# A transformer block in one kernel: the first token loads split over two queues, key rows set by GpSimd, the second root's order, and the last output columns in two parts

## The chip, the cores and the metric

The kernel runs on one core of a Trainium2 chip. A core has five engines that run side by side and wait for each other through semaphores: TensorE (PE; its weight loads are listed as PEld), VectorE (DVE), ScalarE (ACT), GpSimd (POOL) and SyncE (SP), which here only issues transfers. SP and ACT each have a DMA queue of their own. The metric is the device time of one execution in microseconds.

## The reference

The input x has 2048 tokens of 512 values. Two branches read its layer norm: attention over a sliding window, and a gated feed-forward network. The output is x plus the product of the first and the silu of the second.

```python
xn = _layernorm(x)                                # over the 512 values of a token
qkv = (xn @ wqkv)                                 # 32 heads of 16, window of 256 tokens
s = softmax(mask(q @ k.T / 4)) @ v  @ wo
h = silu(xn @ w1) * (xn @ w3)                     # 1792 wide
g = silu(h @ w2)
out = x + s * g
```

## The kernel before

The 2048 tokens are worked in four tiles of 512. Every float32 matrix is split into a high and a low float16 part, and a product is made of three float16 matmuls (high by high, high by low, low by high); weights are first scaled per matrix by a power of two that comes from their sum of squares. Scores and values work on small PE tiles, the feed-forward part on 128x128 tiles.

What runs when is decided in two steps. The Python code writes all instructions in one order. Then `listed` takes them as a list, estimates how long each takes, and gives every engine (PE, DVE, ACT, POOL, SP) an order of its own; the instructions up to `tc.settled`, which is set after the first projections, keep their written order on PE, DVE and ACT. So a change at the start moves instructions of the other engines in many later places, and PE's hardly at all, since its stream follows the written blocks.

The opening, before the dense stream begins, is what the change touches. Four blocks of 128 tokens (slots 0 to 3) are loaded, blocks 0 and 2 on SP's queue, 1 and 3 on ACT's, and behind them SP issues the first weights: the key part and the query part for the first eight heads (L386), the same for the next eight, the value weights (L346) and gate and up weights (L943). PE runs 22 dummy matmuls meanwhile (`keep_busy`, L1499). For each block DVE takes the statistics (`gather0`, L483, and `average0`, L486); for two blocks together ACT takes a root and DVE its reciprocal (`root01`, `invert01`, `root23`, `invert23`: L511, L515, L516, L517) and DVE refines it (L520, L521). `centre0` (L525) subtracts the mean and scales, `turn0` (L541) transposes on PE, and ACT and DVE make the parts XH and XL of it (L546, L551). For the first weights ACT squares the key part and then the query part with a sum along each row (`square`, L403), POOL casts the sums (L406), PE adds them over the partitions (`add_squares`, L420), DVE makes the scale (`inverse`, L425 to L427), and ACT makes the high parts (L410, the tile whi). With XH and whi the first real matmuls begin (`project`, L652). The second eight heads' weights take the same way by L249, L261, L276, L287, L294, L297 and L322; the value weights by L249, L251, L322 and L323 (wvh, wvl) to L619.

The KA tiles hold the keys of a tile, with rows of a constant; before, DVE fills KA[0], ACT fills KA[1] by one activation (L1476), and POOL fills KA[2] (L1491). At the very end `total_by_columns` makes the last 128 tokens' output in two halves of 256 columns: twelve matmuls each (L1321), then two DVE operations (L1323, L1324) and a store (L1325).

Transfers tell of their landing by eight semaphores, DMAHW0 to DMAHW7, that the compiled program uses in turn: an issue whose semaphore is still in use by a transfer eight places earlier waits until that one has landed.

Of the kernel before, what the change touches and what calls it, by code (L numbers as in the profile page):

```python
# [10 lines left out]
F32 = mybir.dt.float32  # L11
# [3 lines left out]
AF = mybir.ActivationFunctionType  # L15
# [6 lines left out]
P = 128  # L22
# [9 lines left out]
TW = S // NT  # L32
# [14 lines left out]
ONE = 2.0**12  # L47

TWO_ONES = struct.unpack("f", struct.pack("ee", -ONE, -ONE))[0]
# [44 lines left out]
def tile_block(ctx: ExitStack, tc: tile.TileContext, x, wqkv, wo, w1, w3, w2, out):  # L94
    nc = tc.nc
    x = x.flatten_outer_dims()
# [26 lines left out]
    def take(dtype):  # L123
        free.sort()
        slot = free.pop(0)[2]
        made = fpool.tile([P, 512 if dtype == F32 else 1024], dtype, name=slot, tag=slot, bufs=1)
        held[id(made)] = slot, made
        return made

    def give(*tiles, after=0):  # L130

        for made in tiles:
            given[0] += 1
            free.append((now[0] + after, given[0], held.pop(id(made))[0]))
# [38 lines left out]
    def bank(shape, dtype=F32):  # L173

        open_bank[0] = b = 1 - open_bank[0]
        return psm.tile(shape, dtype, name=f"m{b}", tag=f"m{b}", bufs=1)
# [24 lines left out]
    onesb = const.tile([P, P], BF16, name="onesb")  # L201
# [30 lines left out]
    KA = [const.tile([P, 4, KW], F16, name=f"KA{r}") for r in range(3)]  # L232
# [235 lines left out]
    def prepare(t):  # L468
# [3 lines left out]
        xts = {}  # L472
        pair = [None]

        def load(b):
            xts[b] = take(F32)
            (nc.scalar if t == 0 and b % 2 else nc.sync).dma_start(xts[b], x[t * TW + b * P:t * TW + (b + 1) * P, :])

        sts = {}

# [75 lines left out]
        def turn_beside(b, k0, k1, s, at=WIN):  # L556
# [17 lines left out]
            def rest():  # L574
# [5 lines left out]
                if whole:  # L580
                    turned[t] = turned.get(t, 0) + 1
            return rest
        return load, (gather, average) if t == 0 else stats, rstd if t == 0 else rstd_beside, centre, turn if t == 0 else turn_beside

    def prepare_beside(t, more=0):
# [659 lines left out]
    def gated(t, b):  # L1245


        if (t, b) in ACC and not isinstance(ACC[t, b], list):
            acc = ACC[t, b]
            y = take(F32)  # L1250
            nc.scalar.activation(y, acc, AF.Tanh, scale=0.5)
            nc.vector.scalar_tensor_tensor(y, y, 1.0, acc, op0=ALU.add, op1=ALU.mult)
            give(acc)
            return [y[:, 0:256], y[:, 256:512]], [y]
        h = b // 2
        if b % 2 == 0:
            GATED[t, h] = []
            for acc in HALF.pop((t, h)):
                y = take(F32)
                nc.scalar.activation(y, acc, AF.Tanh, scale=0.5)  # L1260
                nc.vector.scalar_tensor_tensor(y, y, 1.0, acc, op0=ALU.add, op1=ALU.mult)
                give(acc)
                GATED[t, h].append(y)
        ys = GATED[t, h]
        return [y[:, 256 * (b % 2):256 * (b % 2) + 256] for y in ys], ys if b % 2 else []
# [44 lines left out]
    def total_by_columns(t, b):  # L1310

        r = slice(t * TW + b * P, t * TW + (b + 1) * P)
        tb = slice(b * P, (b + 1) * P)
        WOH, WOL = SQ["wo"][:2]
        xr = XR[t, b]
        ys, done = gated(t, b)
        for c, y in zip((slice(0, 256), slice(256, 512)), ys):
            ps = bank([P, 256])
            for g in range(NG):
                for i, (a, w) in enumerate(((0, WOH), (0, WOL), (1, WOH))):  # L1320
                    nc.tensor.matmul(ps, O[t, g][:, a, tb], w[g][:, c], start=g == 0 and i == 0,  # L1321
                                     stop=g == NG - 1 and i == 2)
            nc.vector.scalar_tensor_tensor(y, ps, sc["y"], y, op0=ALU.mult, op1=ALU.mult)  # L1323
            nc.vector.tensor_add(y, y, xr[:, c])  # L1324
            nc.sync.dma_start(out[r, c], y)  # L1325
        give(*done, xr)
# [140 lines left out]
    load0, stats0, rstd0, centre0, turn0 = prepare(0)  # L1467
# [3 lines left out]
    for b in range(4):  # L1471
# [1 line left out]

    nc.scalar.activation(KA[1][:, 0, 0:1], eps, AF.Sqrt, bias=eps)
    nc.vector.memset(KA[0].rearrange("p a c -> p (a c)").bitcast(F32), TWO_ONES)
    nc.scalar.activation(KA[1].rearrange("p a (b c) -> p (a b) c", c=P), onesb.unsqueeze(1).to_broadcast([P, 24, P]),  # L1476
                         AF.Copy, scale=-ONE)
    qk[0][0]()
    qk[1][0]()
    wv[0]()  # L1480
# [6 lines left out]
    load(0, 3)  # L1487

    nc.gpsimd.memset(V[:, :, H * VW:], 0.0)
    for a in range(4):  # L1490
        nc.gpsimd.memset(KA[2][:, a, :].bitcast(F32), TWO_ONES)  # L1491


    spare = pso.tile([P, 2, TW], F32, name="po")
# [6 lines left out]
    gather0, average0 = stats0  # L1501
    root01, invert01, refine01 = rstd0(0, 2)
    root23, invert23, refine23 = rstd0(2, 4)
# [8 lines left out]
    root01()  # L1512
    gather0(2)
    invert01()
    square(0)
    gather0(3)
    average0(2)
    average0(3)
    root23()
    square(1)  # L1520
    refine01()
    centre0(0)
    copies.append(turn0(0))
    invert23()
    add_squares()
    centre0(1)
    copies.append(turn0(1))
    copies[0][0]()
    refine23()
# [69 lines left out]
    for n in range(len(units)):  # L1599
        t = n // 8  # L1600
# [7 lines left out]
        b = n % 8 - (2 if t == 1 else 4)  # L1608
# [28 lines left out]
    for b in range(4):  # L1637
        if b < 2:
            residual(NT - 1, b + 2)
        if b < 3:  # L1640
            run(total(NT - 1, b))
    total_by_columns(NT - 1, 3)
    flush()

# [419 lines left out]
```

## Time and profile before

| what | value |
|---|---|
| median of 3 runs (lowest, highest) | 793.35 us (793.29, 794.3) |
| the profiled execution's own time | 793.33 us |
| its span in the profile | 791.5 us |
| PE busy | 784.8 us, 99% of the span |
| DVE, ACT, POOL busy | 563.0, 453.3, 383.0 us |
| granted clock of PE over the span | 1.00 |
| moved by DMA | 121.94 MB, mean 154 GB/s |

The span runs from the first to the last instruction; 1.83 us of the profiled time lie around it. A row of the timeline reads: start in us, duration in us, engine, line, operation, out<-in, shape, count, and in brackets how long the engine had been idle and who ended that. A queue's own instructions are SPq and ACTq. An engine that is 99% busy here leaves 6.7 us that are not PE's, and they lie at the two ends.

### The profile page before, as it was taken

The numbers are of one execution on the slowest core, as the hardware profiler recorded it, in microseconds if no ns is written. First come the engines' busy times: TensorE is split into PE (matmuls) and PEld (weight loads), VectorE is DVE, ScalarE is ACT, GpSimd is POOL, SyncE is SP. The second block draws the span as 40 slices with busy tenths as digits, with TensorE's granted clock in tenths as the row PEclk, the third lists the DMA queues.
The fourth block names the chain that finished last, engine by engine and source line by source line (L and its number), as shares of the span: only waits on it lengthen the run. The fifth ranks groups of instructions, "written<-read, shape, count | busy, mean of one in ns | idle before, by whom it ended". The sixth has DMA issues, their size and how long they took to land.

```text
span 791.5 us, 23612 instructions
## 1 busy us (share of the span) xinstructions
PE 784.8 (99%) x9292; PEld 420.6 (53%) x9292; DVE 563.0 (71%) x1348; ACT 453.3 (57%) x754; POOL 383.0 (48%) x679
## 2 busy tenths in 40 slices
PE   8999999999999999999999999999999999999998
PEld 4444445444455554465556555445555555545554
DVE  8787787689667767788668766776767777676536
ACT  7999989757447655544354455644434356654411
POOL 2258858967527334516144633423152456544352
PEclk9999999999999999999999999999999999999999
DMA  9988775474863643556454543527464564225521
GB/s 285 278 242 230 244 216 163 122 206 138 249 174 111 166 133 87 150 163 156 125 148 127 168 117 98 141 66 184 123 178 124 146 180 113 59 93 169 166 68 54
DMA packets 112752, 121.94 MB, mean 154 GB/s; under 512 B 18432, under 2 KB 76928, under 8 KB 112640
## 3 DMA queue, kind: packets, MB, share of 16 engines
q1 hardware_dynamic: 112352, 119.90, 53.9%
q8 instruction: 73, 1.20, 0.7%
q10 hardware_dynamic: 288, 0.52, 0.2%
q14 instruction: 39, 0.32, 0.1%
HBM read 83.76 MB, written 32.37 MB: 147 GB/s over the span
## 4 chain that ended last, share of the span: by engine, by line
PE 95%; ACT 3%; DMA 1%; DVE 1%; issue 0%; SPq 0%; POOL 0%; ACTq 0%
PE m L1105 36%; PE m L1208 11%; PE m L652 10%; PE po L872 9%; PE m L1155 6%; PE s L844 6%; PE m L619 5%; PE m L1286 5%; PE po L752 2%; PE s L752 2%; DMA slot<-in_A_wqkv_dram 1%; PE s L706 1%; ACT slot L331 1%; PE s L652 1%; ACT slot L332 1%; ACT pt L854 1%
## 5 line engine op out<-in xcount | busy, mean ns | idle before, releaser
L1105 PE MATMUL m<-XH,slot 128*128 128x512 f16 x896 | 267.3, 380 | 0.0
L854 ACT ACTIVATE pt<-s,es 128x1024 f32<-128x1024 f32 x152 | 167.1, 1113 | 125.8 <-DVE s L851 124.0
L1105 PEld LDWEIGHTS <-slot 128*128 128x128 f16 x1344 | 125.0, 98 | 149.4 <-issue 9.2
L328 POOL TENSOR_TENSOR slot<-slot,slot 128x256 f16<-128x256 f32 (+1 forms) x222 | 150.0, 701 | 94.7 <-ACT slot L332 37.4
L1105 PE MATMUL m<-XL,slot 128*128 128x512 f16 x448 | 169.8, 379 | 0.0
L851 DVE TENSOR_TENSOR s<-s,MK 128x256 f32<-128x256 f32 (+2 forms) x280 | 119.3, 436 | 67.4 <-PE s L844 57.6
L1074 POOL TENSOR_TENSOR slot<-slot,slot 128x256 f16<-128x256 f32 x133 | 86.2, 671 | 49.7 <-ACT slot L1070 47.3
L1208 PE MATMUL m<-slot,slot 128*128 128x256 f16 x798 | 94.0, 273 | 0.0
L1208 PEld LDWEIGHTS <-slot 128*128 128x128 f16 x798 | 75.8, 98 | 15.1 <-issue 3.2
L872 PE MATMUL po<-pt,V 64*32 64x320 f32 (+4 forms) x2880 | 77.7, 344 | 0.0
L872 PEld LDWEIGHTS po<-pt,V 64*32 64x32 f32 x2880 | 51.8, 106 | 23.7 <-PE s L752 3.3
L1125 DVE SCALAR_TENSOR_TENSOR slot<-m,slot 128x512 f32<-128x512 f32 x56 | 38.4, 685 | 28.6 <-PE m L1105 28.4
L1116 ACT ACTIVATE slot<-m,sgs 128x512 f32<-128x512 f32 x56 | 38.4, 685 | 34.5 <-PE m L1105 34.4
L844 PEld LDWEIGHTS <-KA 50*64 50x64 f16 x1472 | 34.1, 106 | 42.7 <-issue 38.7
L1070 ACT CAST slot<-slot 128x512 f16<-128x512 f32 (+1 forms) x76 | 41.8, 565 | 24.3 <-DVE slot L1125 19.7
L844 PE MATMUL s<-qa,KA 50*64 50x320 f16 (+3 forms) x1472 | 53.9, 258 | 0.4 <-ACT pt L854 0.4
L1120 DVE SCALAR_TENSOR_TENSOR slot<-slot,m 128x512 f32<-128x512 f32 x56 | 38.2, 682 | 19.9 <-ACT slot L1116 18.3
L1155 PE MATMUL m<-slot,slot 128*128 128x512 f16 x216 | 49.2, 380 | 0.0
L652 PE MATMUL m<-XH,whi 128*128 128x512 f16 (+1 forms) x124 | 44.9, 374 | 0.3 <-ACT whi L322 0.3
L652 PE MATMUL m<-XH,wlo 128*128 128x512 f16 (+1 forms) x124 | 44.7, 372 | 0.0
L652 PE MATMUL m<-XL,whi 128*128 128x512 f16 (+1 forms) x124 | 44.7, 372 | 0.0
L735 POOL TENSOR_TENSOR NM<-M,NM 128x16 f16<-128x16 f32 x32 | 7.0, 217 | 76.8 <-ACT NM L734 71.2
(219 smaller groups left out, 1193.2 us busy)
## 6 DMA issues: line engine op xcount, KB each, us to landing
slot<-dW SPq DMA_DIRECT2D x88, 256.0 KB
slot<-dR SPq DMA_DIRECT2D x56, 256.0 KB
slot<-in_B_w_dram SPq DMA_DIRECT2D x42, 256.0 KB
dW<-slot SPq DMA_DIRECT2D x32, 256.0 KB
slot<-in_A_x_dram SPq DMA_DIRECT2D x30, 256.0 KB
KA<-dK SPq DMA_DIRECT2D x24, 288.0 KB
dR<-slot SPq DMA_DIRECT2D x49, 128.0 KB
qa<-dQ SPq DMA_DIRECT2D x32, 192.0 KB
```

What stands on the lines that cost most here:

```text
L328: op(out[:, c], a[:, c], b[:, c])
L619: nc.tensor.matmul(pv, a[:, c, tok], b[c], start=c == 0 and i == 0, stop=c == NC - 1 and i == 2)
L652: nc.tensor.matmul(cell["pp"][:, q], a[:, k, c, :], b[:, c, q], start=(q, c, i) == same[0], stop=(q, c, i) == same[-1])
L844: nc.tensor.matmul(s[64 * h:64 * h + 64, r, o:o + 64 * n], ka[rows, 2 * p + a, 64 * (m + 4):64 * (m + 5)], qa[rows, 2 * p + a, 64 * (m + k ...
L851: nc.vector.tensor_add(v, v, MK[:, kind, of:of + n, :].unsqueeze(1).to_broadcast([P, 2 * len(which), n, 64]))
L854: nc.scalar.activation(pt, s, AF.Exp, scale=es)
L872: nc.tensor.matmul(cell["po"][32 * i:32 * i + 32, h, 64 * (m + k):64 * (m + k + n)], V[64 * h:64 * h + 64, (4 * t + m // 2) % VB, hd * VW: ...
L1070: nc.scalar.copy(made[:, c], raw[:, c])
L1074: nc.gpsimd.tensor_sub(made[:, D + c.start:D + c.stop], raw[:, c], made[:, c])
L1105: nc.tensor.matmul(cell[k], w[:, (a * NC + c) * P:(a * NC + c + 1) * P], b[:, c, :], start=c == 0 and i == 0, stop=c == NC - 1 and i == 2)
L1155: nc.tensor.matmul(ps, hh[:, a * TW + b * P:a * TW + (b + 1) * P], w[:, c * D:(c + 1) * D], start=f == f0 and i == 0, stop=f == f1 - 1 and ...
L1208: nc.tensor.matmul(ps[:, blk, :], l[:, a * D + q:a * D + q + 128], r[:, 256 * c:256 * c + 256], start=f == f0 and x == 0, stop=f == f1 - 2 ...
```

## The change

Four edits. (1) Each of the first four token blocks is loaded as two halves of 64 tokens, one on SP's queue and one on ACT's. (2) ACT's fill of KA[1] goes, and POOL fills it as it fills KA[2], with four memsets more. (3) The last steps of the second root (`invert23`) are written ahead of `centre0(0)` and of the second `square`, which itself goes behind `centre0(0)`; `gather0(3)` goes ahead of the first `square`. (4) The last block's columns 256 to 511 are made in two parts of 128.

```diff
-            (nc.scalar if t == 0 and b % 2 else nc.sync).dma_start(xts[b], x[t * TW + b * P:t * TW + (b + 1) * P, :])
+            r = t * TW + b * P
+            if t == 0:
+                nc.sync.dma_start(xts[b][0:64], x[r:r + 64, :])
+                nc.scalar.dma_start(xts[b][64:P], x[r + 64:r + P, :])
+            else:
+                nc.sync.dma_start(xts[b], x[r:r + P, :])
...
-        for c, y in zip((slice(0, 256), slice(256, 512)), ys):
-            ps = bank([P, 256])
+        for c, y in ((slice(0, 256), ys[0]), (slice(256, 384), ys[1][:, 0:128]), (slice(384, 512), ys[1][:, 128:256])):
+            ps = bank([P, c.stop - c.start])
...
-    nc.scalar.activation(KA[1].rearrange("p a (b c) -> p (a b) c", c=P), onesb.unsqueeze(1).to_broadcast([P, 24, P]),
-                         AF.Copy, scale=-ONE)
...
-    for a in range(4):
-        nc.gpsimd.memset(KA[2][:, a, :].bitcast(F32), TWO_ONES)
+    for r in (1, 2):
+        for a in range(4):
+            nc.gpsimd.memset(KA[r][:, a, :].bitcast(F32), TWO_ONES)
...
     invert01()
+    gather0(3)
     square(0)
-    gather0(3)
     average0(2)
     average0(3)
     root23()
+    refine01()
+    invert23()
+    centre0(0)
     square(1)
-    refine01()
-    centre0(0)
     copies.append(turn0(0))
-    invert23()
+    centre0(1)
     add_squares()
-    centre0(1)
     copies.append(turn0(1))
```

The diff doesn't tell all that moves. On SP's queue, at the program's beginning, the rows before were these (slots 166 and 170 are token blocks 0 and 2, 178 the first key weights, 177 the first query weights; in brackets the landing semaphore that the issue waits for):

```order
L477 DMA slot_166<-in_A_x_dram 128x512
L477 DMA slot_170<-in_A_x_dram 128x512
L386 DMA slot_178<-in_A_wqkv_dram 128x4x128
L386 DMA slot_177<-in_A_wqkv_dram 128x4x128
L386 DMA slot_181<-in_A_wqkv_dram 128x4x128
L386 DMA slot_182<-in_A_wqkv_dram 128x4x128
L346 DMA slot_185<-in_A_wqkv_dram 128x512 [waits DMAHW0_49]
```

And now (slots 166, 169, 172 and 175 are the blocks, 181 the first key weights):

```order
L479 DMA slot_166<-in_A_x_dram 64x512
L479 DMA slot_169<-in_A_x_dram 64x512
L479 DMA slot_172<-in_A_x_dram 64x512
L479 DMA slot_175<-in_A_x_dram 64x512
L386 DMA slot_181<-in_A_wqkv_dram 128x4x128 [waits DMAHW0_49]
L386 DMA slot_180<-in_A_wqkv_dram 128x4x128 [waits DMAHW1_49]
```

Eight halves now take all eight semaphores, so the first key weights, issued without a wait before, wait for a half of block 0 to land.

On DVE, from the end of the first refinement (`rs` by L521) on, before (the slots are blocks 0 and 1):

```order
L521 SCALAR_TENSOR_TENSOR rs<-sq,rs 128x2
L525 TENSOR_SCALAR slot_166<-slot_166,mv,rs 128x512
L515 RECIPROCAL r_225<-sq 128x2
L516 TENSOR_TENSOR sq<-r_225 128x2
L525 TENSOR_SCALAR slot_168<-slot_168,mv,rs 128x512
```

And now (L526 was L521, L520 was L515, L521 was L516, L530 was L525):

```order
L526 SCALAR_TENSOR_TENSOR rs<-sq,rs 128x2
L520 RECIPROCAL r_232<-sq 128x2
L521 TENSOR_TENSOR sq<-r_232 128x2
L530 TENSOR_SCALAR slot_166<-slot_166,mv,rs 128x512
L530 TENSOR_SCALAR slot_169<-slot_169,mv,rs 128x512
```

The reciprocal of the second root now stands ahead of the first block's centring; likewise on ACT the copy `rs` of it (L517) now stands between that root and the second square (L403), where it stood behind the square.

The list moves more behind the first projections. On ACT, at the second eight heads' weights, before (squares of two weights of 128x512 each and two value weights, then the high part whi for the key weights in slot 182):

```order
L249 ACTIVATE sqa,ssq<-slot_181 128x512
L249 ACTIVATE sqa,ssq<-slot_182 128x512
L249 ACTIVATE sqa,ssq<-slot_185 128x512
L249 ACTIVATE sqa,ssq<-slot_186 128x512
L322 ACTIVATE whi_410<-slot_182,sw_381 128x512
L661 ACTIVATE slot_422<-s 128x512
L322 ACTIVATE whi_410<-slot_181,sw_381 128x512
```

And now (slot 199 is a gate weight, L666 was L661):

```order
L249 ACTIVATE sqa,ssq<-slot_184 128x512
L249 ACTIVATE sqa,ssq<-slot_185 128x512
L249 ACTIVATE sqa,ssq<-slot_188 128x512
L249 ACTIVATE sqa,ssq<-slot_189 128x512
L249 ACTIVATE sqa,ssq<-slot_199 128x512
L666 ACTIVATE slot_429<-s 128x512
L322 ACTIVATE whi_417<-slot_185,sw_388 128x512
L322 ACTIVATE whi_417<-slot_184,sw_388 128x512
```

A fifth square and the copy of the first projection now stand ahead of whi. On PE the four small matmuls that add the value weights' squares (L276) moved from behind the eight matmuls that use this whi to ahead of them; further on PE's order differs in a handful of blocks.

## The prediction

> **What bounds the kernel now.** I read the page's head first, then PE's waits, then the chain of waits and the timeline of the opening, and last the end.
>
> ```profile
> span 791.5 us, 23612 instructions
> PE 784.8 (99%) x9292; PEld 420.6 (53%) x9292; DVE 563.0 (71%) x1348; ACT 453.3 (57%) x754; POOL 383.0 (48%) x679
> ...
> PE m L541 <- DVE r L515: 0.7, 1, 0.7
> PE s L844 <- ACT pt L854: 0.4, 1, 0.4
> PE m L652 <- ACT whi L322: 0.3, 1, 0.3
> ...
> 0.00:10.00 10.00, 8.09 (x29) 3.27 (x30) 7.05 (x26) 6.75 (x12) 4.61 (x24) 1.00 0.84 263
> ```
>
> PE is the bound from the first projection to the last. Its waits behind the start are 0.7, 0.4 and 0.3 us, so no edit can win much in the middle. What can move is the moment when the real stream begins, the waits in the first 30 us, and the tail behind the last matmul; a delay in the opening goes through to the end, since the 0.4 us is all that a later wait could swallow. PE's 8.09 busy us in the first ten are mostly the dummies. The opening in order of time (the first row is of the chain of waits, the rest of the timeline):
>
> ```profile
> 1.63 6.26 DMA slot<-in_A_wqkv_dram
> ...
> 0.72 0.86 SPq L477 DMA_DIRECT2D slot<-in_A_x_dram  x2
> 1.07 7.36 PE L1499 MATMUL po<-onesb 128*128 128x512 bf16 x22 [1.07 <-DVE onesb L202]
> 3.27 2.76 ACT L1476 ACTIVATE KA<-onesb 128x3072 f16<-128x3072 bf16 x1
> 4.49 1.29 DVE L483 BATCH_NORM_STATS2 st<-slot 128x6 f32<-128x512 f32 x2 [1.49 <-DMA slot<-in_A_x_dram]
> 6.03 0.30 ACT L511 ACTIVATE sq<-mv,eps 128x2 f32<-128x2 f32 x1
> 6.11 1.82 PEld L1499 LDWEIGHTS <-onesb 128*128 128x128 bf16 x9 [0.22 <-issue]
> ...
> 7.92 0.63 ACT L403 ACTIVATE sqa<-slot 128x512 bf16<-128x512 f32 x1 [0.82 <-DMA slot<-in_A_wqkv_dram]
> ...
> 8.26 0.16 DVE L521 SCALAR_TENSOR_TENSOR rs<-sq,rs 128x2 f32<-128x2 f32 x1
> ...
> 8.46 0.55 DVE L525 TENSOR_SCALAR slot<-slot,mv,rs 128x512 f32<-128x512 f32 x1
> 8.54 0.28 ACT L511 ACTIVATE sq<-mv,eps 128x2 f32<-128x2 f32 x1
> 8.88 0.63 ACT L403 ACTIVATE sqa<-slot 128x512 bf16<-128x512 f32 x1
> 8.92 0.16 DVE L515 RECIPROCAL r<-sq 128x2 f32<-128x2 f32 x1
> ...
> 9.15 0.63 PE L541 MATMUL m<-identf,slot 128*128 128x128 f32 x4 [0.72 <-DVE r L515]
> 9.19 0.54 DVE L525 TENSOR_SCALAR slot<-slot,mv,rs 128x512 f32<-128x512 f32 x1
> 9.51 0.19 ACT L517 ACTIVATE rs<-r 128x2 f32<-128x2 f32 x1
> 9.67 0.18 POOL L406 CAST sb<-ssq 128x2 bf16<-128x2 f32 x1 [4.53 <-ACT sqa L403]
> ...
> 10.93 0.15 DVE L427 TENSOR_SCALAR sw<-al 128x1 int32<-128x1 int32 x1
> 11.12 1.34 ACT L410 ACTIVATE whi<-slot,sw 128x512 f16<-128x512 f32 x2
> 11.90 0.61 PE L652 MATMUL s<-XH,whi 128*128 128x256 f16 x4
> ```
>
> Two lines of work meet at 11.90. Tokens: statistics, roots, centring, transposes. Weights: the key part lands, ACT squares it at 7.92, and everything behind hangs on that. ACT sat idle 0.82 us for this landing, and the second root (8.54) is queued behind that square. So the landing, W = 7.9 us, sets both lines.
>
> **Tokens by halves: no gain as long as W stands.** Block 0 has two halves in flight side by side instead of sharing with block 1. How the bytes flowed (40 slices of 0.25 us):
>
> ```profile
> GB/s 0 0 0 0 0 0 0 49 172 164 254 393 319 393 393 393 434 393 373 354 279 293 293 314 301 305 301 309 311 318 307 299 309 334 291 348 357 397 369 391
> ...
> SPq L346 <- DMA slot<-in_A_x_dram: 0.2, 1, 0.2
> ```
>
> Summed, 0.26 MB were through at 3.0 us, 0.52 MB (two blocks) at 3.75, 1.05 MB (all four) at 5.1. DVE began on the pair at 4.49, 0.74 us behind its bytes; so block 0 alone should begin at about 3.0 + 0.74 = 3.75, and the first two averages come 0.6 us earlier. Blocks 2 and 3 land no earlier. Refinement ended at 8.42 and may now end by 8.0, but the second root still stands behind the first square, and so behind W.
>
> The Trainium skill, "DMA: Bandwidth & Descriptors", section "Issuing engines are not separate DMA queues", speaks against this edit: transfers started by different engines run on the same 16 DMA engines, and only the issuing time is saved. By that rule W is not earlier, and the sum stays +1.2 us; if the edit did bring more bytes through, W could move by the 1.1 us worked out below, and the sum would be +0.1.
>
> W itself: key weights (0.26 MB) were through by bytes at 6.0 us, 1.9 us before the square, against 0.74 us for tokens. If only 0.74 remained, W = 6.75, a gain of 1.15: the lower end. The other way: the issue was free at 1.63; now it waits for a half of block 0, at about 3.75 by the estimate above (that issues do wait so shows in SP's wait for a token block). The first issue at 0.72 had bytes moving at about 1.85, 1.1 us later, so key bytes start at about 4.9, just before the tokens run out at 5.1. If the ramp is paid again (1.75 to 2.75 moved at 160 GB/s instead of 390) it is 0.6 us late: the upper end. I take 0, since the bytes meet without a gap.
>
> **GpSimd's four memsets: 0.** ACT's fill ended at 6.03, when the root began; gone, the root can go earlier, but see above. POOL has nothing to do until 9.67, four memsets of about 0.4 us fit, and without that cover they would cost 1.6.
>
> **The second root: +0.45.** The root can't start before 8.54, so its reciprocal stays at 8.92. Before, DVE centred block 0 at 8.46, in that very wait; now centring waits for the reciprocal and its square and starts at 9.19, where block 1's stood: block 0 is 0.73 late. Block 1 follows one centring later (0.55, of which the next operation overlaps 0.1, as 8.92 does 9.01), at 9.64, 0.45 late. Everything on DVE behind it, through L427, goes 0.45 later: whi at 11.57. On ACT the copy waits for the reciprocal (9.08) and takes 0.19, so the second square starts near 9.3 rather than 8.88, POOL's cast near 10.1; this 0.4 is covered by DVE's 0.45. PE begins at 12.35 instead of 11.90. Bounds: 0 if the root comes early because W does; 0.75 if block 0's delay is not caught up.
>
> Here PE's gap before the first transpose grows from 0.7 to about 1.4 us. The nine last dummies loaded weights in 1.82 us, 0.20 each; the 13 before took 6.11 - 1.07 = 5.0 us, 0.39 each: the array started at half speed, and could fall back. Half speed for the 5 us that it took to speed up would cost 2.5; I take 0. The Trainium skill, "TensorE: Matmul & The Clock Gate", "The HAM clock gate", puts the fall at an idle window of about 3.4 us; by it the gap costs nothing, and the sum is +1.2 rather than +3.7.
>
> **What the list moved: +0.75.** The second heads' key weights:
>
> ```profile
> 16.42 0.63 ACT L249 ACTIVATE sqa<-slot 128x512 bf16<-128x512 f32 x1
> ...
> 17.55 0.72 ACT L322 ACTIVATE whi<-slot,sw 128x512 f16<-128x512 f32 x1 [0.40 <-DVE sw L297]
> ...
> 18.18 0.58 ACT L661 ACTIVATE slot<-s 128x512 f16<-128x512 f32 x1
> ...
> 18.32 1.04 PE L652 MATMUL m<-XH,whi 128*128 128x512 f16 x4 [0.27 <-ACT whi L322]
> ...
> 20.06 0.24 PE L276 MATMUL s<-sb,onesb 128*128 128x1 bf16 x4
> ...
> 22.37 2.74 DVE L323 SCALAR_TENSOR_TENSOR wvl<-slot,swwv,wvh 128x512 f16<-128x512 f32 x4
> ...
> 23.82 1.29 PE m L619 x6
> ```
>
> Before, ACT was free at 17.15 (0.40 before 17.55), so a square takes 0.73. Now a fifth takes it to 17.9, the copy L661 goes next, and whi starts 0.5 behind that, at 18.4 instead of 17.55: PE's eight matmuls move from 18.32 to 19.2, and PE already waited there. That is 0.87. Taken back is L276, now in the wait: 0.24 as recorded, about half of it over the matmul before. Net +0.75, on top of the 0.45. Bounds 0.4 (ACT's lateness partly caught up) and 1.0. On DVE two more operations of 128x512 now stand ahead of wvl (0.69 each by L323's 2.74/4), so it begins near 22.37 + 0.45 + 1.4 = 24.2, and its first quarter is done near 24.9; PE, at 23.82 + 1.2 = 25.0, wants it one matmul later (1.29/6 = 0.2). That is 0, with 0.5 as its other end.
>
> **The last columns: 0.**
>
> ```profile
> 787.05 0.42 DVE L1324 TENSOR_TENSOR slot<-slot,slot 128x256 f32<-128x256 f32 x1
> 787.70 0.48 DVE L1323 SCALAR_TENSOR_TENSOR slot<-m,us,slot 128x256 f32<-128x256 f32 x1 [0.22 <-PE m L1321]
> 788.22 0.42 DVE L1324 TENSOR_TENSOR slot<-slot,slot 128x256 f32<-128x256 f32 x1
> ...
> L851 DVE TENSOR_TENSOR s<-s,MK 128x256 f32<-128x256 f32 x3 | 1.3, 427 | 0.7 <-PE s L844 0.7
> ...
> L851 DVE TENSOR_TENSOR s<-s,MK 128x128 f32<-128x128 f32 x3 | 0.9, 299 | 0.1
> ```
>
> Half the width saves 0.13 us of an operation, not half. DVE is free at 787.47; then four operations of 0.35, 0.29, 0.35 and 0.29 with their 0.03 gaps end at about 788.75, against 788.64 before. PE's twelve matmuls more carry half the columns each, so its end hardly moves. The last store carries half the bytes. I take 0, from -0.2 to +0.2.
>
> **The sum.** 0 + 0 + 0.45 + 0.75 + 0 = +1.2 us. The profiled execution took 793.33 us (791.5 and 1.83 around it), within 0.02 of the median 793.35, so I forecast 794.6, with 794.0 to 795.2 as this case's own range. A measurement of this kernel can tell about 0.2%, 1.6 us, from no change.
>
> **The rivals.** *The key weights land early.* For it: the 1.9 us between bytes and square, against 0.74. W would be 6.8 to 7.2 and the opening, 0.45 less 0.7 to 1.1, 0.3 to 0.6 earlier than before, which pays for half of the 0.75: +0.3, 793.65. With everything favourable (-0.65, the whi wait of 0.3 and the later one of 0.4 gone, 0.2 at the end) -1.6, the edge of what counts as faster. Against: nothing in the edit shortens a transfer of 512-byte pieces.
>
> *The key weights land late*, the rival on the slower side. Their issue waits for a landing, and the DMA engines run dry and ramp again: W = 8.3 to 8.5, and each 0.1 us goes through to the end. +1.8, with DVE's wvl wait up to +2.3: 795.4. It decides over the 0.2% from W = 8.3 on. For it: the new wait, only 0.2 us in hand. Against: bytes of tokens still flow then.
>
> *The clock falls back* in the longer gap: up to +3.7, 797. Against: a gap of 0.7 did nothing before, and 1.4 is short beside the 5 us that speeding up took. The granted clock says 1.00 for the slow dummies too, so the spacing of matmuls would have to show it.
>
> *The change doesn't do what it says*: the order shows that it does, except that halves in the end give DVE more to do than they save.
>
> **How the numbers follow.** My forecast has 0.50, of which 0.08 lies above 1.6 us; early weights 0.19, of which 0.05 at -1.6 and below; late weights 0.27; the clock 0.04. Faster 0.05, same 0.42 + 0.14 = 0.56, slower 0.08 + 0.27 + 0.04 = 0.39. The range leaves out the clock, the last of the late case and the most favourable: 793.1 to 796.2.
>
> **What would show it.** Right: the first square still at about 7.9, the first transpose near 9.9, first projections near 12.35, a PE wait of about 1 us for whi near 19, last DVE end near 788.7 plus the shift. Wrong: a first square before 7.4 or after 8.3, matmuls at twice their spacing behind 12 us, or PE waits behind 50 us that weren't there before.

## The result, and the profile after

The changed kernel takes 794.7 us (median of 22 runs, 793.78 to 796.23), the kernel before on the same chip 793.19 (22 runs): ratio 1.0016, 95% interval 1.001 to 1.0022. That is 0.1 us from the forecast of 794.6. Several terms of the sum were nevertheless wrong.

One thing must be known to read the times: each run lists its mean granted TensorE clock. In 12 of the 22 runs it is 0.999 or 1.0, with a median of 794.12; in 10 it is 0.997 or 0.998, with a median of 795.09. The kernel before, in 84 runs beside the experiments, has 70 of the first sort (793.21) and 14 of the second (794.37). "Clock kept" and "clock lost" below mean these two. So the change costs 0.9 us where the clock is kept, and makes its loss, worth about 1.0 us, more frequent.

The profiled execution of the changed kernel kept its clock and took 794.15 us. First the head of its page, then PE's waits:

```profile
span 792.2 us, 23647 instructions
PE 784.6 (99%) x9304; PEld 420.8 (53%) x9304; DVE 562.1 (71%) x1350; ACT 449.8 (57%) x753; POOL 385.8 (49%) x683
```

```profile
PE m L546 <- issue: 1.6, 1, 1.6
...
PE m L657 <- ACT whi L322: 0.6, 1, 0.6
...
PE s L276 <- DVE sb L261: 0.2, 1, 0.2
```

PE's work is the same; its pause ahead of the first transpose has grown from 0.7 to 1.6 us and the wait for the second heads' weights from 0.3 to 0.6. The timeline of the changed kernel, in order of time (start, length, engine, line, operation, count, in brackets the idle time before it and what ended it):

```profile
0.71 2.50 ACTq L480 DMA_DIRECT2D slot<-in_A_x_dram  x4
0.72 2.77 SPq L479 DMA_DIRECT2D slot<-in_A_x_dram  x4
1.07 7.58 PE L1503 MATMUL po<-onesb 128*128 128x512 bf16 x22 [1.07 <-DVE onesb L202]
...
3.53 2.92 SPq L386 DMA_DIRECT2D slot<-in_A_wqkv_dram  x4
...
3.98 0.69 DVE L488 BATCH_NORM_STATS2 st<-slot 128x6 f32<-128x512 f32 x1 [0.98 <-DMA slot<-in_A_x_dram]
...
5.69 0.69 DVE L488 BATCH_NORM_STATS2 st<-slot 128x6 f32<-128x512 f32 x1 [1.02 <-DMA slot<-in_A_x_dram]
...
6.30 0.30 DVE L491 BATCH_NORM_AGGREGATE mv<-st 128x2 f32<-128x6 f32 x2
...
7.59 0.69 DVE L488 BATCH_NORM_STATS2 st<-slot 128x6 f32<-128x512 f32 x1
...
8.35 0.63 ACT L403 ACTIVATE sqa<-slot 128x512 bf16<-128x512 f32 x1 [0.64 <-DMA slot<-in_A_wqkv_dram]
...
8.98 0.28 ACT L516 ACTIVATE sq<-mv,eps 128x2 f32<-128x2 f32 x1
9.29 0.17 DVE L520 RECIPROCAL r<-sq 128x2 f32<-128x2 f32 x1 [0.25 <-ACT sq L516]
...
9.57 1.00 DVE L530 TENSOR_SCALAR slot<-slot,mv,rs 128x512 f32<-128x512 f32 x2
...
10.21 0.63 PE L546 MATMUL m<-identf,slot 128*128 128x128 f32 x4 [1.57 <-issue]
...
11.79 0.15 DVE L427 TENSOR_SCALAR sw<-al 128x1 int32<-128x1 int32 x1
11.97 1.33 ACT L410 ACTIVATE whi<-slot,sw 128x512 f16<-128x512 f32 x2
...
12.75 0.61 PE L657 MATMUL s<-XH,whi 128*128 128x256 f16 x4
...
18.03 0.63 ACT L249 ACTIVATE sqa<-slot 128x512 bf16<-128x512 f32 x1
18.09 0.68 DVE L251 CUSTOM_DVE_ANT_0 junk<-slot 128x512 bf16<-128x512 f32 x1
...
18.66 0.58 ACT L666 ACTIVATE slot<-s 128x512 f16<-128x512 f32 x1
...
18.70 0.15 DVE L297 TENSOR_SCALAR sw<-al 128x1 int32<-128x1 int32 x1
...
19.14 1.32 ACT L322 ACTIVATE whi<-slot,sw 128x512 f16<-128x512 f32 x2
...
19.90 1.04 PE L657 MATMUL m<-XH,whi 128*128 128x512 f16 x4 [0.55 <-ACT whi L322]
...
789.33 0.29 DVE L1329 TENSOR_TENSOR slot<-slot,slot 128x128 f32<-128x128 f32 x1
```

Set beside the rows of before: the key weights are asked for at 3.53 instead of 1.63, since SP spends 2.77 us on four halves (0.69 each) where two whole blocks took 0.86 (0.43 each); first square 8.35 for 7.92, first transpose 10.21 for 9.15, first projections 12.75 for 11.90 (+0.85), second heads' projections 19.90 for 18.32 (+1.58). With PE's matmuls of the two traces matched one to one, the delay is 0.85 from 9 to 18 us, 1.44 after the moved matmuls of L276, 1.62 from 24 us (a wait for the value weights' low part), then falls to 1.13 by 50 us, where small gaps of the kernel before are no longer there; it is 1.23 from 140 us on and 1.00 from 655 us. DVE ends at 789.62 instead of 788.64 (+0.98), and from there to the end of the span it is 2.6 us instead of 2.9, so the span grows by 0.7 to 0.8.

### The profile page after: what moved, and what is told of

It is laid out like the page before. It is cut to its first block, busy times and chain, and to the rows that moved or that the text cites. A ratio compares the mean times of both kernels' runs of the same rounds, so it can differ in the third digit from the quotient of the medians.

```text
span 792.2 us, 23647 instructions
## 1 busy us (share of the span) xinstructions
PE 784.6 (99%) x9304; PEld 420.8 (53%) x9304; DVE 562.1 (71%) x1350; ACT 449.8 (57%) x753; POOL 385.8 (49%) x683
## 4 chain that ended last, share of the span: by engine, by line
PE 96%; DVE 1%; ACT 0%; issue 0%; ACTq 0%
PE m L1110 37%; PE m L1213 11%; PE m L657 10%; PE po L877 10%; PE m L1160 6%; PE s L849 6%; PE m L624 5%; PE m L1291 5%; PE po L757 2%; PE s L757 2%; PE s L711 1%; PE s L572 1%; PE po L711 0%; PE s L657 0%; PE s L624 0%; PE m L1326 0%
## 5 line engine op out<-in xcount | busy, mean ns | idle before, releaser
L1110 PE MATMUL m<-XH,slot 128*128 128x512 f16 x896 | 267.3, 380 | 0.1
L1110 PEld LDWEIGHTS <-slot 128*128 128x128 f16 x1344 | 125.0, 98 | 149.8 <-issue 10.1
L1110 PE MATMUL m<-XL,slot 128*128 128x512 f16 x448 | 169.8, 379 | 0.0
L1075 ACT CAST slot<-slot 128x256 f16<-128x256 f32 (+1 forms) x76 | 41.5, 566 | 20.7 <-DVE slot L1130 14.9
```

Of the source, the lines that this page charges most:

```text
L1075: nc.scalar.copy(made[:, c], raw[:, c])
L1110: nc.tensor.matmul(cell[k], w[:, (a * NC + c) * P:(a * NC + c + 1) * P], b[:, c, :], start=c == 0 and i == 0, stop=c == NC - 1 and i == 2)
```

## The experiments

All were timed beside the kernel before; the table gives them in order. The last columns are of one profiled execution each: starts of the first square, first transpose and first projections. An "h" marks projections that ran under half the clock, which makes them late for that reason too.

| kernel | runs | median us | clock kept: runs, median | clock lost: runs, median | square | transpose | projections |
|---|---|---|---|---|---|---|---|
| before (first profile) | 84 | - | 70, 793.21 | 14, 794.37 | 7.92 | 9.15 | 11.90 |
| changed | 22 | 794.70 | 12, 794.12 | 10, 795.09 | 8.35 | 10.21 | 12.75 |
| halves_only | 5 | 797.63 | 2, 797.33 | 3, 797.80 | 8.48 | 10.27 | 13.63h |
| no_halves | 8 | 795.11 | 4, 794.50 | 4, 795.77 | 7.01 | 9.30 | 11.79 |
| root_back | 11 | 794.47 | 7, 794.12 | 4, 795.40 | 8.39 | 9.79 | 13.56h |
| dummies28 | 11 | 794.53 | 11, 794.53 | 0 | 8.23 | 10.09 | 12.63 |
| root_only | 11 | 793.19 | 8, 793.13 | 3, 794.30 | 6.96 | 9.25 | 11.89h |
| pool_only | 11 | 793.33 | 9, 793.15 | 2, 794.35 | 7.01 | 9.15 | 11.90 |
| cols_only | 11 | 793.03 | 10, 793.02 | 1, 794.13 | 6.95 | 9.10 | 12.41h |
| half_block0 | 11 | 795.30 | 3, 794.47 | 8, 795.56 | 7.75 | 9.97 | 12.79h |
| before_again | 1 | 793.41 | 1, 793.41 | 0 | 7.06 | 9.20 | 11.95 |
| halves_pool | 11 | 795.03 | 4, 794.34 | 7, 795.38 | 8.30 | 10.12 | 12.92 |
| before_dummies16 | 11 | 794.37 | 7, 793.84 | 4, 794.86 | 6.86 | 9.01 | 11.76 |
| root_cols | 11 | 792.90 | 11, 792.90 | 0 | 6.87 | 9.16 | 11.66 |

### Halves alone, halves taken back, root taken back, longer warm-up

**halves_only.** Edit 1 on the kernel before.

```diff
-            (nc.scalar if t == 0 and b % 2 else nc.sync).dma_start(xts[b], x[t * TW + b * P:t * TW + (b + 1) * P, :])
+            r = t * TW + b * P
+            if t == 0:
+                nc.sync.dma_start(xts[b][0:64], x[r:r + 64, :])
+                nc.scalar.dma_start(xts[b][64:P], x[r + 64:r + P, :])
+            else:
+                nc.sync.dma_start(xts[b], x[r:r + P, :])
```

> The kernel before with the token halves alone. Theory 1 (each half costs its queue 0.6 to 0.8 us of issuing where a whole block cost 0.4, so the key weights are asked for later): the first square at 8.3 to 8.4 instead of 7.92, the first projections at about 12.35 instead of 11.90 although the root stands where it stood, a fifth square ahead of the second heads' weights and a PE wait of 0.5 to 0.6 us for them, time about 794.2 (+0.4 for the landing, +0.6 for the weights of the second heads). Rival A (the halves cost nothing, the second root's order makes the loss): first square at 7.9, first projections at 11.9, only the +0.6 of the fifth square, 793.8. Rival B (the whole median loss is a granted clock that falls back in the long pause of PE): pause near 1.1 us instead of 1.6, so clock 1.0 in nearly all runs.

Measured: 797.63 us, ratio 1.0056 (1.0043 to 1.0069). First square at 8.48, a fifth square ahead of the second heads' weights, and a wait of 1.0 us for them. The sizes of all theories were too small; rival B's clock of 1.0 in nearly all runs isn't there either (3 of 5 lost it), and the two runs that kept it are 4 us above the kernel before. Two rows of its timeline show what else the halves push:

```profile
4.87 2.76 ACT L1481 ACTIVATE KA<-onesb 128x3072 f16<-128x3072 bf16 x1
...
7.54 0.28 ACT L516 ACTIVATE sq<-mv,eps 128x2 f32<-128x2 f32 x1
```

ACT issues four halves before anything else, so its fill starts 1.6 us late and holds the first root until 7.54 instead of 6.03. With the matmuls matched to before, 2.1 of the delay of 4.6 us in this profile arise behind 100 us, in waits spread over the program: every edit of the opening lays the later instructions of ACT, DVE and POOL anew.

**no_halves.** The changed kernel with the `dma_start` line of before (the diff above the other way round).

> The changed kernel with whole token blocks again. Theory 1: first square back at 7.9, no fifth square ahead of the second heads' weights, first projections at 12.3 to 12.4 (the order of the second root alone, +0.45), time 793.5 to 793.7, of which the end gives 0.2 back. Rival A (the root's order carries the loss): first projections at 12.7 and 794.2 or more. Rival B (the clock): the pause of PE ahead of the first transpose is about 1.2 us; if that is enough for a fall, the runs fall into two groups about 1 us apart as those of the changed kernel do.

Measured: 795.11 us, ratio 1.0023 (1.0013 to 1.0034); clock kept 794.50. The opening is *better* than before (11.79), so theory 1's +0.45 for the order of the root isn't there, and the time with the clock kept is still 0.8 above theory 1's. The runs do fall into two groups, as rival B says, 4 and 4. Its waits and timeline say where:

```profile
PE m L652 <- ACT whi L322: 0.9, 1, 0.9
...
PE s L706 <- ACT pt L854: 0.7, 1, 0.7
```

```profile
16.99 0.69 DVE L251 CUSTOM_DVE_ANT_0 junk<-slot 128x512 bf16<-128x512 f32 x1
...
17.55 0.60 ACT L661 ACTIVATE slot<-s 128x512 f16<-128x512 f32 x1 [0.51 <-PE s L652]
...
17.87 0.15 DVE L297 TENSOR_SCALAR sw<-al 128x1 int32<-128x1 int32 x1
...
18.05 1.33 ACT L322 ACTIVATE whi<-slot,sw 128x512 f16<-128x512 f32 x2
...
18.83 1.04 PE L652 MATMUL m<-XH,whi 128*128 128x512 f16 x4 [0.88 <-ACT whi L322]
```

There is no fifth square on ACT here, and the wait for whi is there all the same. The list did two things. It put a DVE square of 0.69 us between two steps of the shift `sw`, which so ends at 18.02; and it put the copy L661, which waits for PE, ahead of whi on ACT, where it stood behind it, so that ACT is free at 18.05. Either alone would have brought whi to about this time. Another order elsewhere made a new wait of 0.7. In the changed kernel both stand again, beside the fifth square: DVE's at 18.09, between L294 and L297, and the copy (L666) at 18.66; there `sw` ends at 18.85, and whi follows the copy at 19.14.

**root_back.** The changed kernel with squares, second root and centring written as before.

```diff
-    gather0(3)
     square(0)
+    gather0(3)
...
-    refine01()
-    invert23()
-    centre0(0)
     square(1)
+    refine01()
+    centre0(0)
     copies.append(turn0(0))
-    centre0(1)
+    invert23()
     add_squares()
+    centre0(1)
```

> The changed kernel with the first squares, the second root and the centring in the order of before. Theory 1 and the prediction's own term: DVE centres block 0 about 0.7 earlier, the first transpose comes 0.7 earlier, the first projections 0.45 earlier at about 12.3; the first square stays at 8.3; time of the undisturbed runs 793.6, or 0.45 below the changed kernel. Rival A': the root's order costs nothing because everything waits for the key weights, first projections stay at 12.7 and the time stays. Rival B (the clock): the pause of PE shrinks from 1.6 to about 0.9 us, so the slower group of runs, which shows a granted clock below 1, goes away and the median comes 1 us lower than the changed kernel's.

Measured: clock kept 794.12, exactly the changed kernel's 794.12. The first transpose does come 0.42 earlier (9.79), but not the time. So also with late key weights the order of the root costs nothing that the time shows; `sw` (L427) comes at 11.72 instead of 11.79. Its profile caught a lost clock; the warm-up matmuls and first transpose in its timeline, and the stretches of 1 us after them (PE, PEld, DVE, ACT, POOL busy, granted clock, DMA share, GB/s):

```profile
1.07 6.24 PE L1503 MATMUL po<-onesb 128*128 128x512 bf16 x22 [1.07 <-DVE onesb L202]
...
9.79 0.63 PE L546 MATMUL m<-identf,slot 128*128 128x128 f32 x4 [2.48 <-issue]
```

```profile
10.00:11.00 1.00, 0.55 (x7) 0.37 (x5) 0.75 (x4) 1.00 (x4) 0.19 (x1) 0.80 1.08 374
11.00:12.00 1.00, 1.00 (x7) 1.00 (x6) 0.93 (x5) 0.13 (x1) 0.00 (x0) 0.50 1.05 385
...
13.00:14.00 1.00, 1.00 (x5) 0.42 (x4) 0.66 (x1) 1.00 (x3) 0.00 (x0) 0.50 1.20 300
14.00:15.00 1.00, 1.00 (x11) 0.94 (x10) 1.00 (x3) 0.39 (x1) 0.00 (x0) 0.99 1.22 291
```

The same 22 warm-up matmuls took 6.24 us here and 7.58 in the changed kernel's profile: the clock came up earlier, PE ran dry at 7.31, and the pause was 2.5 us. Then the clock was granted at 0.50 for 0.4 + 3.0 + 0.0 = 3.4 us, in the middle of the first projections. The expectation that a shorter pause removes this was wrong as put (4 of 11 lost it, against 10 of 22).

**dummies28.** The changed kernel with more warm-up.

```diff
-    keep_busy(22)
+    keep_busy(28)
```

> The changed kernel with 28 instead of 22 warm-up matmuls ahead of the first transpose, which keep PE busy until about 9.9 us. Rival B (in about half of the runs the granted clock falls back in the 1.6 us pause and costs about 1 us): no run with a granted clock below 1, all runs at 793.8 to 794.3, median 0.5 us or more below the changed kernel's 794.7. Theory 1 alone (delay only, the clock has nothing to do with the pause): two groups as before, median 794.7. If the warm-up matmuls end later than the first transpose could start, up to +0.2.

Measured: PE's pause shrinks to 0.3 us, and none of 11 runs lost the clock. That is what rival B said of the clock and theory 1 denied. The median was to fall by 0.5 and only falls to 794.53, since the kept-clock runs are 0.4 slower than the changed kernel's; the list was laid anew, and a wait of 0.5 us (`m L1110`) came in. The new list also has no fifth square ahead of whi, only the copy:

```profile
19.64 1.04 PE L657 MATMUL m<-XH,whi 128*128 128x512 f16 x4 [0.42 <-ACT whi L322]
```

That is 7.01 us behind the first projections (12.63), where the changed kernel has 7.15 and the kernel before 6.42. So the fifth square makes 0.14 of the delay.

### Each edit alone, and halves for one block

Beside the four kernels of this group the kernel before had a median of 793.29 with the clock kept (28 of its 84 runs), beside the others 793.18. So differences of 0.1 us between kernels of different groups say nothing.

**root_only.** Edit 3 on the kernel before (the diff of root_back the other way round); PE's order is unchanged.

> The kernel before with the second root and the first squares in the order of the changed kernel, nothing else; PE's instructions keep their order. Theory 1 (the prediction's term): first transpose about 9.9 instead of 9.15, first projections about 12.35 instead of 11.90, so 793.6 in undisturbed runs (+0.45). Theory 2 (the grid of the clock: the granted clock is set anew every 3.4 us from how busy PE was in the 3.4 us before; PE's pause now runs to 9.9): a third to a half of the runs show a granted clock of 0.998 or less and lie 0.8 to 1.2 us higher, where the kernel before has 3 of 24. Rival A': no change of the first projections, because the key weights set them: 793.2 and 1 run in 8 disturbed.

Measured: 793.19, ratio 0.9999 (0.999 to 1.0008), clock kept 793.13. First transpose at 9.25, not 9.9. The term of +0.45 is 0, or 0.1 to 0.2 to the good. 3 of 11 runs lost the clock, fewer than theory 2 said; the transpose was hardly later, so the pause wasn't either.

**pool_only.** Edit 2 on the kernel before.

```diff
-    nc.scalar.activation(KA[1].rearrange("p a (b c) -> p (a b) c", c=P), onesb.unsqueeze(1).to_broadcast([P, 24, P]),
-                         AF.Copy, scale=-ONE)
...
-    for a in range(4):
-        nc.gpsimd.memset(KA[2][:, a, :].bitcast(F32), TWO_ONES)
+    for r in (1, 2):
+        for a in range(4):
+            nc.gpsimd.memset(KA[r][:, a, :].bitcast(F32), TWO_ONES)
```

> The kernel before with the 24-block fill of ACT replaced by four memsets of GpSimd, nothing else by hand (the list of the later instructions is laid anew). The prediction's term: 0, because the root behind the fill waits for the key weights' square anyway. Rival C: without the fill of 2.76 us the key weights land earlier, as they did in the kernel with whole blocks (6.7 instead of 7.9): first projections up to 0.6 earlier, 792.6 to 793. Rival D (the luck of the list): the opening unchanged, but waits of 0.2 to 1 us elsewhere because some 200 instructions of ACT and POOL are laid in another order; 793.0 to 794.5.

Measured: 793.33, ratio 0.9999 (0.999 to 1.0008), clock kept 793.15. Nothing, as predicted. But the first square stood at 7.01, 0.9 earlier than in the first profile of before, and the first projections at 11.90 all the same. That contradicts the prediction's picture of the opening.

**cols_only.** Edit 4 on the kernel before.

```diff
-        for c, y in zip((slice(0, 256), slice(256, 512)), ys):
-            ps = bank([P, 256])
+        for c, y in ((slice(0, 256), ys[0]), (slice(256, 384), ys[1][:, 0:128]), (slice(384, 512), ys[1][:, 128:256])):
+            ps = bank([P, c.stop - c.start])
```

> The kernel before with the last 256 columns in two parts, nothing else; the other instructions keep nearly all their places. The prediction's term: 0, last DVE end at 788.75 (+0.1) and the last store half as large. Theory 1 from the two traces: DVE's end -0.0 to +0.1, from there to the end of the span 2.58 instead of 2.82 us, so 793.0 (-0.2). Rival: DVE's two operations more and PE's twelve matmuls more cost 0.3 at the end: 793.4.

Measured: clock kept 793.02 against 793.21 (793.29 beside it), so -0.2 to -0.3, where theory 1 said -0.2; the ratio's interval (0.9984 to 1.0002) still holds 1. Its profile lost the clock after a pause of 1.8 us, with the first transpose at 9.10. The kernel before loses the clock too, in 14 of 84 runs.

**half_block0.** The changed kernel, halves for block 0 only.

```diff
-            if t == 0:
+            if t == 0 and b == 0:
                 nc.sync.dma_start(xts[b][0:64], x[r:r + 64, :])
                 nc.scalar.dma_start(xts[b][64:P], x[r + 64:r + P, :])
             else:
-                nc.sync.dma_start(xts[b], x[r:r + P, :])
+                (nc.scalar if t == 0 and b % 2 else nc.sync).dma_start(xts[b], x[r:r + P, :])
```

> The changed kernel with only block 0 of the tokens loaded by halves; blocks 1 to 3 whole on the queues of before. Theory 1 (the price of the halves is their number of issues on each queue): each queue issues one piece more than before (+0.2 to +0.4 us), so the key weights' first issue at about 2.0 instead of 3.53, landing at 7.9 or earlier, first projections 12.3 to 12.4, no fifth square ahead of the second heads' weights, 793.6 in undisturbed runs, and a part of the runs higher by about 1 us from the clock. Rival A (the root's order alone makes the opening late): first projections at 12.75 as in the changed kernel, 794.1.

Measured: 795.30, ratio 1.0022 (1.0013 to 1.0031), clock kept 794.47. The key weights' first issue came at 2.22 and the first square at 7.75, as theory 1 said, and there was no fifth square; yet the time missed by 0.9. The statistics of the last block began at 7.69, where before_again below has 7.03, and `sw` (L427) came at 11.54. So one block by halves already holds up the blocks behind it, which counting issues on each queue doesn't explain: that theory fell.

### A second look at before, and what beats it

**before_again.** The kernel before, unchanged.

> The kernel before once more, unchanged, for a second profile. Theory 3 (the key weights do not set the opening: DVE's own row of operations from the last block's statistics to the shift does, and the landing at 7.89 in the first profile was late by chance): weights land near 6.75 as in the four other kernels with whole blocks, first square near 7.0, and all the same the first transpose at 9.15, the first projections at 11.90 and 793.2. Rival (the prediction's): the landing is at 7.9 again, and 11.90 hangs on it.

Its timeline:

```profile
7.03 0.69 DVE L483 BATCH_NORM_STATS2 st<-slot 128x6 f32<-128x512 f32 x1
7.06 0.61 ACT L403 ACTIVATE sqa<-slot 128x512 bf16<-128x512 f32 x1
...
7.96 0.30 ACT L511 ACTIVATE sq<-mv,eps 128x2 f32<-128x2 f32 x1 [0.20 <-DVE mv L486]
...
8.51 0.55 DVE L525 TENSOR_SCALAR slot<-slot,mv,rs 128x512 f32<-128x512 f32 x1
...
9.20 0.63 PE L541 MATMUL m<-identf,slot 128*128 128x128 f32 x4 [1.28 <-DVE r L515]
...
10.98 0.15 DVE L427 TENSOR_SCALAR sw<-al 128x1 int32<-128x1 int32 x1
...
11.95 0.61 PE L652 MATMUL s<-XH,whi 128*128 128x256 f16 x4
```

The square runs without a wait at 7.06, 0.86 before its time in the first profile, and everything behind stays: centring 8.51 for 8.46, transposes 9.20 for 9.15, projections 11.95 for 11.90. Theory 3 holds. The landing at 7.9 was a late one, that the six other kernels with whole blocks didn't show either (squares at 6.86 to 7.01), and nothing hung on it. What sets the opening is DVE's own row, from the last block's statistics (7.03) through averages, refinements, centrings to `sw` (10.98), in which the profile shows no wait of DVE. The bytes that feed this row, in stretches of 1 us, first of before_again:

```profile
3.00:4.00 1.00, 1.00 (x3) 0.30 (x2) 0.00 (x0) 0.97 (x2) 1.00 (x5) 1.00 0.93 356
4.00:5.00 1.00, 1.00 (x4) 0.42 (x3) 0.45 (x1) 1.00 (x1) 1.00 (x5) 1.00 1.04 396
```

and then of the changed kernel:

```profile
3.00:4.00 1.00, 1.00 (x3) 0.29 (x2) 0.02 (x2) 0.75 (x1) 0.94 (x6) 1.00 0.89 197
4.00:5.00 1.00, 1.00 (x4) 0.41 (x3) 0.68 (x1) 0.83 (x2) 1.00 (x6) 1.00 0.78 256
```

356 and 396 GB/s against 197 and 256. Here the halves lose what they were to win.

**halves_pool.** Edits 1 and 2 on the kernel before (the diffs of halves_only and pool_only).

> The kernel before with the token halves and GpSimd's four memsets, without the new order of the root and without the new last columns. Theory: of the 4 us that the halves alone lost, the part behind the pause comes from ACT's fill of 2.76 us, which the four issues on ACT's queue push from 3.27 to 4.87 and which then holds the first root until 7.54; without the fill the root is at 6.0 to 6.7, the first transpose near 9.8 rather than 10.27, and undisturbed runs at 794 to 795. Rival (the luck of the list): the opening is as in the changed kernel and later waits still bring it to 796 or more.

Measured: 795.03, ratio 1.0022 (1.0013 to 1.003), clock kept 794.34 against halves_only's 797.33. The first root came at 7.03 instead of 7.54. So GpSimd's memsets, worth nothing alone, are worth 3 us beside the halves, in the opening and through the list together; how much is each wasn't separated.

**before_dummies16.** The kernel before with less warm-up.

```diff
-    keep_busy(22)
+    keep_busy(16)
```

> The kernel before with 16 instead of 22 warm-up matmuls; the first transpose stays near 9.15, so PE's pause grows from 0.7 to 1.9 us (or from 2.0 to 3.2, where the clock came up early). Theory 2 (the granted clock is set anew every 3.4 us, up where PE was busy for over about 60% of the last 3.4 us, down where it was busy for under about half): 8 of 10 runs or more show a clock of 0.998 or less, where the kernel before has 8 of 57, and lie 0.5 to 1.2 us higher. Rival (a fall needs 3.4 us of idle time without a break): no fall in any run, since the pause stays under 3.4 us, and 793.2 to 793.5.

Measured: 794.37, ratio 1.0009 (1.0001 to 1.0018); 4 of 11 lost the clock. Neither forecast holds: not 8 in 10, and not none. Its profile kept the clock through a pause of 1.6 us; the last section says why that doesn't speak against theory 2's "about half". With the clock kept its runs are 0.6 above the kernel before (793.84). The list put DVE's square ahead of `sw` here too, with the copy behind whi and no fifth square, and PE's wait for the second heads' weights is 0.8 us:

```profile
17.89 0.72 ACT L322 ACTIVATE whi<-slot,sw 128x512 f16<-128x512 f32 x1 [0.89 <-DVE sw L297]
```

**root_cols.** Edits 3 and 4 on the kernel before (the diffs of root_only and cols_only).

> The kernel before with the changed order of the second root and the last columns in two parts, without halves and without GpSimd's memsets. Theory: the order gives 0.1 and the columns 0.2, so undisturbed runs at 792.9, the lowest of all, with 1 to 3 runs in 11 higher by 1.1 us from the clock. Rival: the two do not add, 793.1.

Measured: 792.90, 11 runs from 792.81 to 793.44, none with the clock lost; ratio 0.9993 (0.9984 to 1.0002). Its runs are the lowest of all kernels, 1.8 us under the changed kernel, and its gain over before, 0.3 us by the kept-clock medians, is about the sum of the two edits alone (0.1 and 0.2 by the same medians, 0.2 and 0.3 against the runs beside them); the interval of the ratio doesn't quite exclude 1. It also shows the luck of the list: no_halves differs from it by edit 2 alone, which by itself is worth nothing, and takes 1.6 us more with the clock kept (794.50). In the two profiles, matched as above, only 0.13 of this lies ahead of 18 us; the rest comes in behind, with the waits shown under no_halves.

## Why the prediction was right, and where its steps were not

The total was right in good part by luck: wrong terms offset each other, and half of the runs lost the clock, which the sum had left out.

**"The landing W sets both lines": this step failed.** It rested on one late landing in one profile and on ACT's 0.82 us of idleness. In before_again the landing is out of the way, and nothing moves. The row that should have warned: block 0 was centred at 8.46, straight behind `rs` at 8.26, in DVE's queue, and the transposes at 9.15 followed from that, not from the square.

**The second root, +0.45: mis-sized, it is 0 to -0.1.** It hung on the failed step: with the first square at 6.9 to 7.1 it is done before the second root's input is there (7.96), and the root is not queued behind it. DVE has the same operations to do in another order. root_only (793.13 kept against 793.21) and root_back (794.12 against 794.12) show it with early and with late weights.

**Tokens by halves, 0: mis-sized, about +1.** First projections: 12.75 against 11.79 without the halves, +0.96. The step said that the first two averages would come 0.6 us earlier and that the key weights' bytes would follow the tokens' without a gap. Block 0 did come earlier (DVE began at 3.98 instead of 4.49), but DVE then waited 1.02 us for block 1, and the averages came at 6.30, 0.6 later. The rows of before:

```profile
5.69 0.30 DVE L486 BATCH_NORM_AGGREGATE mv<-st 128x2 f32<-128x6 f32 x2
...
6.97 0.69 DVE L483 BATCH_NORM_STATS2 st<-slot 128x6 f32<-128x512 f32 x1
```

Each half cost its queue 0.69 us on SP and 0.63 on ACT instead of 0.43 and 0.45, and the bytes thinned out. The key weights' issue, which the prediction let wait for a landing, came at 3.53 straight behind SP's fourth half, and their square at 8.35. Of the +0.85 against before, 0.62 are there when the last block's statistics begin (7.59 instead of 6.97), and 0.25 is DVE's wait at 9.29 for the second root, which in this kernel does stand behind the late square (8.98). So the rival "late weights", with its 795.4, had the sign right and the place for the smaller share; that the tokens come later was in neither the forecast nor a rival. For the other possibility, that the halves win bytes, nothing was found. The Trainium skill ("DMA: Bandwidth & Descriptors", "Issuing engines are not separate DMA queues") says that transfers started by different engines run on the same 16 DMA engines and that a second issuer saves issuing time alone; the trace agrees in so far as no bytes were won (197 and 256 GB/s). The same section calls that time usually small beside the transfer. Here SP took 2.77 us to issue four halves, 0.52 MB, which at the 356 GB/s of before_again take about 1.5 us (an estimate).

**GpSimd's memsets, 0:** right alone (793.15 against 793.21). Not foreseen was that they pay for the halves by clearing ACT.

**The list, +0.75: right in size.** Measured 1.58 - 0.85 = 0.73 at the matmuls, 0.59 after the matmuls of L276. The cause was named only in part. The fifth square makes 0.14 (dummies28). The copy that now stands ahead of whi ends last in the changed kernel, and DVE's square ahead of `sw`, which the prediction doesn't have, comes close behind it; before_dummies16 has that square alone and a wait of 0.8, no_halves has square and copy and a wait of 0.9. The value weights' low part cost 0.17, within the 0 to 0.5 given.

**The end and the middle.** Last columns: predicted 0 from -0.2 to +0.2, measured -0.2 alone. Not in the sum: 0.5 us are regained by 50 us and 0.2 at 655, in gaps that the kernel before had. By terms, with the clock kept: 0.85 + 0.59 + 0.17 - 0.48 + 0.10 - 0.23 - 0.24 = +0.76, where the two profiled executions differ by 0.82.

**The clock, chance 0.04: under-rated.** It fell in 10 of 22 runs, and cost 1.0 us, not the 2.5 that were set as a bound. The argument was that a gap of 0.7 us "did nothing before", read from a single execution; in 14 of 84 runs of the kernel before the clock was lost. And the gap isn't fixed: the warm-up's end moves with the moment at which the clock comes up. The Trainium skill ("TensorE: Matmul & The Clock Gate", "The HAM clock gate") says that the window is free-running, so that this moment varies from run to run; the runs agree (6.24 to 7.65 us for the same 22 matmuls). It puts the fall behind an idle window of about 3.4 us, and from this the prediction took that a short gap is safe: the fall after 1.8 us in cols_only shows that it isn't. The 3.4 us return as the length of the slow stretch. dummies28, which closes the pause, lost no clock in 11 runs.

With kept clock alone the change would have shown 794.1; the forecast met the median because the lost clock came on top.

## What to carry to other kernels

Before a landing is called the bound, ask whether the operations behind it start when it arrives, or when the queue of another engine lets them; a second profile of the same kernel is the cheapest test. Splitting transfers over two queues multiplies issues, and each piece may cost more to issue than the whole did: cost them, and look at what is queued behind them on both engines. Where a list is laid anew by every edit, an edit's own effect (here 0 to 1 us) and the luck of the list (1.6 us in one pair of kernels) must be told apart by kernels whose order is nearly the same.

## What the runs showed of the hardware

The clock can be lost behind a pause of PE well under 3.4 us, and the length of the pause alone doesn't decide. From the waits of two profiles, the first with the clock lost (cols_only), the second with it kept (halves_pool):

```profile
PE m L541 <- DVE r L515: 1.8, 1, 1.8
```

```profile
PE m L546 <- issue: 1.7, 1, 1.7
```

By the traces' clock records, the five profiles with a lost clock (pauses of 1.7 to 2.9 us) lost it 6.83 us after it had come up, which is twice 3.41, and for 3.41 us; no profile with a pause of 1.3 us or less lost it. Pauses of 1.7 us stand on both sides, in halves_pool and in root_only.

What divides the two is how the pause lies to these steps. Count stretches of 3.41 us from the moment at which the clock came up. In the five, PE was busy for 0.15, 0.22, 0.41, 0.44 and 0.48 of the second stretch, at whose end the clock fell (halves_only, root_back, cols_only, half_block0, root_only). In the nine that kept the clock, no stretch of the opening had less than 0.52 (before_dummies16), and the next lowest was 0.64 (changed). The clock had come up early in the five, at 3.8 to 4.8 us against 5.0 to 6.6 in the nine, and so most of the pause fell into one stretch; halves_pool's 1.7 us are split over two, each busy for 0.70. So in these fourteen profiles the border lies between 0.48 and 0.52; no run varied this share by itself.

Open is why a half costs more to issue than a whole block: with only block 0 halved, its two halves took 0.59 and 0.56 us, and the whole block behind them on SP 0.81.
